# Decoding the input weights at fixed units of the attention loop, value half first

## The chip, the core and the metric

The kernel runs on one core of a Trainium2 chip. Its time is the device time of one execution in microseconds (us). The kernel before took 809.89 us in the median of three runs (809.17 to 810.18).

## What is computed

Attention with a block mask over 4 batches of 8 heads (576 positions, head size 64), then a gated feed-forward with a spatial mixing step, then a normalised second feed-forward with a residual. Only the first product of the second step matters for this change: `x @ w_in`, whose columns are two halves. Columns 0 to 511 give `u`, here called the **gate half**, columns 512 to 1023 give `v`, the **value half**.

```python
def _moe_ref(x, w_in, w_spatial, b_spatial, w_out):
    h = np.maximum(x @ w_in, 0.0)
    u, v = (h[..., :d_ff // 2], h[..., d_ff // 2:])
    ...
    gated = u * v_s
    return (gated @ w_out).astype(np.float32)
```

[...]

## The kernel before

**Units and pairs.** The attention works on 16 pairs of heads, four to a batch, numbered 0 to 15. Each pair is nine units of 64 or 128 query rows: the joint last rows of both heads first (i = 0), then blocks of 512, 384, 256 and 128 key columns, one for each head (i = 1 to 8). The main loop (L513) runs over the unit number u = 9 p + i, so the first batch is u = 0 to 35 and the second u = 36 to 71. A unit traces its score products (L214 and on, three PSUM banks), the mask and row minimum on VectorE (DVE, L275), the exponential on ScalarE (ACT, L282); two units later the transposes of the result on TensorE (PE, L333) and their evictions (DVE L324 for the wide units, ACT L326 for the others). At i = 7 a pair's weighted sum over the first part of the transposes is traced (`pv` from `pH`, L386, 20 matmuls), at i = 2 of the next pair the rest (`pv` from `pL`, 8 matmuls). At i = 0 the reciprocals of the previous pair are traced (DVE L292 and L293, PE L295, ACT L297). From i = 1 on, the next pair's `stack` operands are prepared (DVE L55 or ACT L57, and GpSimd, POOL, L188 or L196 to L202).

**The dense work.** From u = 44 on, the loop also deals out the products `x @ w_in` of the batch before, a few matmuls a unit (`fill`, L488): first four or five tiles of the value half (`vps`, L431), then four blocks of the gate half (`ups`, L462).

**Decoding w_in.** `win` holds `w_in` as a high and a low float32 part, in four row blocks `kc`. `decode_in` (L402) is a generator; each `next` on it traces one of eight parts, 128x512 numbers each: an activation that reads the high words (ACT L87), a shift of the low words (DVE L88), their joining (DVE L89), then a rounding copy (POOL L100) and a subtraction (POOL L101) into `win`. The loop calls it at L536 to L538, at i = 1, 4 and 7 of the first four pairs: the first call (u = 1) starts three fetches, the next eight (u = 4, 7, ... 25) trace the parts, and each part starts the fetch of the third part on (L409, a 512 KB transfer on SyncE's, SP's, queue) into one of three `raw` buffers.

**What sets the order.** The program is traced in source order, but a planner that simulates the engines (`schedule_with_timeline_sim=True`) then chooses each engine's order: an instruction may be brought forward when its inputs are there and its engine is idle in the simulation. `tc.keep_in_program_order` limits this: the instruction is not brought ahead of the one that was traced just before it on its engine. It does not hold back anything that is traced later. `decode` has a parameter `here` for it, which marks L87 and L88; `decode_in` does not use it.

Of the kernel before, what the change touches and what calls it, by code (L numbers as in the profile page):

```python
# [18 lines left out]

PLAN = {'mm': 3, 'sc': 3, 'tr': 2, 'D': 2, 'hi0': 'v', 'hi1': 's', 'klo0': 'g', 'klo1': 'g', 'qlo0': 'g', 'qlo1': 'g', 'xm0': 'g', 'xm1': 'g', 'xh0': 'g', 'xh1': 'g', 'xl0': 'g', 'xl1': 'g', 'dm': 'g', 'dh': 'g', 'ev0': 3, 'ev1': 2, 'rate': 24500.0, 'vrb': 3, 'ds': 2, 'dy': 1, 'raw': 5, 'yn': 2, 'ts': 3, 'ring': 8, 'wt': 2, 'cb': 1, 'hq': 8, 'packed': 4, 'plain': 3, 'pre': 8, 'py': 10, 'pyn': 4, 'dn0': 2, 'dnn': 5, 'vl': 'v', 'pace': 3, 'wd': 7, 'tl0': 'v', 'tl1': 'v', 'xe': 's', 'pt': 6, 'dstart': 8}  # L20


def f32(ap):
    return ap.bitcast(F32)
# [8 lines left out]
def tile_kernel(  # L33
# [26 lines left out]
    NB, NP, _, _, _, S = qk.shape  # L60
    KD = w_in.shape[1]
    DM = 128 * KD
    F = w_in.shape[2] // 2
# [14 lines left out]
    wi32, wo32, w132, w232 = (a.bitcast(U32) for a in (w_in, w_out, w_ch1, w_ch2))  # L78

    def decode(raw, m, e, out, here=lambda ins: ins):  # L80

        low, high = raw[:, :, 0], raw[:, :, 1]
        here(nc.scalar.activation(m, f32(high), AF.Prelu, scale=2.0**-112, alpha=2.0**32))  # L87
        here(nc.vector.tensor_scalar(e, low, 29, None, op0=ALU.logical_shift_right))  # L88
        nc.vector.scalar_tensor_tensor(  # L89
            out.bitcast(U32), m.bitcast(U32), 3, e, op0=ALU.logical_shift_left, op1=ALU.bitwise_or  # L90
        )

    def split(src, hi, lo, high="s", low="g"):

        if high == "s":
            nc.scalar.copy(hi, src)  # L96
        elif high == "v":
            nc.vector.tensor_copy(hi, src)
        else:
            nc.gpsimd.tensor_scalar(hi, src, 1.0, 0.0, op0=ALU.mult, op1=ALU.add)  # L100
        {"v": nc.vector, "g": nc.gpsimd}[low].tensor_tensor(lo, src, f32(hi), op=ALU.subtract)  # L101
# [164 lines left out]
    def softmax(u):  # L266

        j, c = UNITS[u % NU]
        banks = state[u]
        sm = sums[u // NU]  # L270
        pt = at.tile([128, S], F32, tag="p", name="p", bufs=PLAN['pt'])
        nm = at.tile([128, 2], F32, tag="nm", name="nm", bufs=4)
        for i, (s_ps, o, n) in enumerate(banks):
            m = mask[:, 0:n] if c == 4 else mask[:, 512 - n:512]
            nc.vector.tensor_tensor_reduce(  # L275
                pt[:, o:o + n], s_ps[:, :n], m, -0.125, 3e38, ALU.add, ALU.min, nm[:, i:i + 1]
            )
        if c == 4:
            nc.vector.tensor_tensor(nm[:, 0:1], nm[:, 0:1], nm[:, 1:2], op=ALU.min)
        n = o + n  # L280
        col = 8 if c == 4 else 4 * j + c
        nc.scalar.activation(  # L282
            pt[:, :n], pt[:, :n], AF.Exp, bias=nm[:, 0:1], scale=-1.0, accum_out=sm[:, col:col + 1]
        )
        state[u] = (pt, n)
# [31 lines left out]
    def transposes(u):  # L317
        j, c = UNITS[u % NU]
        pt, n = state.pop(u)

        def put(src, dst):
            out = dst(pT_of(u // NU)[1 if c >= 2 else 0])
            if c >= PLAN["ev1" if u >= NU * NP else "ev0"] and not (c == 4 and PLAN["tl1" if u >= NU * NP else "tl0"] == "s"):
                nc.vector.tensor_copy(out, src)  # L324
            else:
                nc.scalar.copy(out, src)  # L326

        def flip(k0, k1):
            tr = p_tr.tile([128, 512], F32, tag="tr", name="tr")
            for kc in range(k0, k1):  # L330
                w = min(128, n - 128 * kc)
                o = 128 * (kc - k0)
                nc.tensor.transpose(tr[:w, o:o + 128], pt[:, 128 * kc:128 * kc + w], idn)  # L333
            return tr

        if c == 4:
            tr = flip(0, 4)
            put(
                tr.rearrange("p (r h q) -> p r h q", h=2, q=64),
                lambda t: view(t, 256, [[WH, 4], [5 * WH, 2], [1, 64]]),  # L340
            )
            tr = flip(4, 5)
            put(
                tr[0:64, 0:128].rearrange("p (h q) -> p h q", q=64), lambda t: t[0:64, :, 4 * WH + 256:5 * WH]
            )
        else:
            tr = flip(0, c + 1)
            put(
                tr[:, :n].rearrange("p (r q) -> p r q", q=128),
                lambda t: view(  # L350
                    t, (5 * WH if c >= 2 else 2 * WL) * j + 128 * (c % 2), [[WH if c >= 2 else WL, c + 1], [1, 128]]
                ),
            )
# [5 lines left out]
    def tick():  # L359
        for e in list(slow):  # L360
            e[0] -= 1
            if e[0] <= 0:
                slow.remove(e)
                e[1]()

    def flush():
        todo, later[:] = list(later), []
        for f in todo:
            f()

    def weighted(p, part):

        flush()
        vt = ops[p][2]
        if p not in xx_t:
            xx_t[p] = at.tile([128, S], F32, tag="xx", name="xx")
        xx = xx_t[p]

        jobs = ((0, 128, 0, WL), (1, 128, 128, WL)) if part == 0 else (
            (0, 128, 0, WH), (1, 128, 0, WH), (2, 128, 0, WH), (3, 128, 128, WH), (4, S - 512, 256, WH))  # L380
        w = WH if part else WL
        src = pT_of(p)[part]
        ps = p_mm.tile([128, 512], F32, tag="mm", name="pv")
        for n, (kc, rows, a, z) in enumerate(jobs):
            for j in (1, 0):
                MM(  # L386
                    ps[64 * j:64 * j + 64, a:z], lhsT=vt[:rows, kc, 64 * j:64 * j + 64],
                    rhs=src[:rows, j, w * kc + a:w * kc + z],
                    start=(n == 0), stop=(n == len(jobs) - 1),
                )  # L390
        later.append(lambda: cp('xe', None, xx[:, 256 * part:256 * part + w], ps[:, :w]))
# [8 lines left out]
        del ops[p]  # L400

    def decode_in():  # L402
        raws = {}

        def fetch(i):
            if i < 2 * KD:
                kc, h = divmod(i, 2)
                raws[i] = dn.tile([128, F, 2], U32, tag="hl", name="raw", bufs=3)
                nc.sync.dma_start(  # L409
                    out=raws[i].rearrange("p a b -> p (a b)"), in_=wi32[:, kc, 2 * F * h:2 * F * h + 2 * F]  # L410
                )

        fetch(0)
        fetch(1)
        fetch(2)
        yield
        for i in range(2 * KD):
            kc, h = divmod(i, 2)
            m = dn.tile([128, F], F32, tag="vr", name="dm", bufs=PLAN["vrb"])
            e = dn.tile([128, F], U32, tag="ur", name="de")  # L420
            cols = slice(F * h, F * h + F)
            decode(raws.pop(i), m, e, m)
            split(m, win[0][:, kc, cols], win[1][:, kc, cols], PLAN['dh'])
            fetch(i + 3)
            yield
# [57 lines left out]
    dense = None  # L483
    debt = 0.0
    dec = decode_in()
    preps = {}

# [22 lines left out]
    size = [200 + (S if c == 4 else 128 * (c + 1)) for _, c in UNITS]  # L510
    tot = float(sum(size) * NP)
    D = PLAN['D']
    for u in range(NS + 8):  # L513
        p, i = divmod(u, NU)
        if u < NS:
            scores(u)
            softmax(u)
        tick()
        flush()
        if D <= u < NS + D:  # L520
            transposes(u - D)
        if i == PLAN['wd'] and p < NPAIR:
            weighted(p, 1)
        if i == 0 and 1 <= p <= NPAIR:
            reciprocals(p - 1)
        if i == D and 1 <= p <= NPAIR:
            weighted(p - 1, 0)
        if i == D + 3 and 1 <= p <= NPAIR:
            store_x(p - 1)
        if i == 0:  # L530
            load(p + 2)
            if p + 1 < NPAIR:
                preps[0] = prepare(p + 1)
        if 0 in preps and i >= 1:
            next(preps[0], None)
        if p < NP:  # L536
            if i % PLAN['pace'] == 1:
                next(dec, None)  # L538
        else:
            b, k = divmod(u, NU * NP)  # L540
            if k == PLAN['dstart'] and b <= NB - 1:
                dense = chain(dense, w_in_stage(b - 1))
            fill(PLAN['rate'] * size[i] / tot)
# [81 lines left out]
    dec = decode_out()  # L625
# [24 lines left out]
    raws = {}  # L650
# [441 lines left out]
def _layout(np, q, k, v, moe_w_in, moe_w_spatial, moe_b_spatial, moe_w_out, moe2_g_ln, moe2_w_ch1, moe2_w_ch2):  # L1092

    B, H, S, D = q.shape
    qk = np.stack([q, k], axis=2).reshape(B, H // 2, 2, 2, S, D).transpose(0, 1, 5, 2, 3, 4)
# [40 lines left out]
```

## Time and profile before

| | us |
|---|---|
| median of three runs | 809.89 |
| lowest and highest | 809.17, 810.18 |
| the profiled execution, its time | 811.71 |
| the profiled execution, first to last instruction | 809.9 |
| PE busy | 790.8 (98%) |
| DVE, ACT, POOL busy | 525.8, 423.9, 415.5 |

The profile lists, for each instruction, its engine, its line, what it writes and reads, when it started, how long it took and, where the engine sat idle before it, what ended that wait. PE is called busy while a matmul is in its pipeline, so a busy PE says little of its pace. The profile also records TensorE's granted clock, as a share of 2.4 GHz; 0.50 is 1.2 GHz. Before the first such record a stretch is shown as 1.00.

### The profile page before, as it was taken

The numbers are of one execution on the slowest core, as the hardware profiler recorded it, in microseconds if no ns is written. First come the engines' busy times: TensorE is split into PE (matmuls) and PEld (weight loads), VectorE is DVE, ScalarE is ACT, GpSimd is POOL, SyncE is SP. The second block draws the span as 40 slices with busy tenths as digits, with TensorE's granted clock in tenths as the row PEclk, the third lists the DMA queues.
The fourth block names the chain that finished last, engine by engine and source line by source line (L and its number), as shares of the span: only waits on it lengthen the run. The fifth ranks groups of instructions, "written<-read, shape, count | busy, mean of one in ns | idle before, by whom it ended". The sixth has DMA issues, their size and how long they took to land.

```text
span 809.9 us, 13259 instructions
## 1 busy us (share of the span) xinstructions
PE 790.8 (98%) x4480; PEld 672.9 (83%) x4480; DVE 525.8 (65%) x1191; ACT 423.9 (52%) x1071; POOL 415.5 (51%) x417
## 2 busy tenths in 40 slices
PE   7999999999999999999999999999999999999998
PEld 4667788868878799899988888889898888988986
DVE  5857655665465196786676788797556578645534
ACT  4678677657665264455363555463345454433431
POOL 5979655655452353232176455564555555545431
PEclk9899999999999999999999999999999999999999
DMA  8645535445342368778620243204001003000002
GB/s 250 179 133 165 155 115 160 142 130 153 110 149 73 114 206 280 233 241 262 205 79 14 79 128 106 80 1 156 1 13 40 1 1 126 18 1 1 1 1 78
DMA packets 53687, 88.66 MB, mean 109 GB/s; under 512 B 6770, under 2 KB 17138, under 8 KB 53620
## 3 DMA queue, kind: packets, MB, share of 16 engines
q1 hardware_dynamic: 53620, 87.83, 35.5%
q8 instruction: 35, 0.57, 0.3%
q14 instruction: 32, 0.26, 0.1%
HBM read 68.85 MB, written 18.95 MB: 108 GB/s over the span
## 4 chain that ended last, share of the span: by engine, by line
PE 84%; DVE 6%; DMA 3%; POOL 2%; issue 2%; ACT 2%; SPq 1%; POOLq 0%; ACTq 0%; DVEq 0%
PE hps L915 21%; PE o L105 8%; PE o L107 8%; PE o L106 8%; PE pv L386 6%; PE tr L333 5%; PE sc L260 4%; PE ups L105 2%; PE by L105 2%; PE by L107 2%; PE by L106 2%; PE sps L107 2%; PE sps L106 2%; PE sps L105 2%; PE ups L106 2%
## 5 line engine op out<-in xcount | busy, mean ns | idle before, releaser
L101 POOL TENSOR_TENSOR a<-s,a 128x256 fp32r<-128x256 f32 x96 | 78.3, 819 | 91.7 <-ACT a L96 91.7
L106 PE MATMUL o<-w,h 128*128 128x512 f32 x288 | 112.9, 393 | 0.0
L275 DVE CUSTOM_DVE_ANT_0 p<-sc,mask 128x256 f32<-128x256 f32 (+4 forms) x160 | 74.0, 472 | 56.8 <-PE tr L333 17.9
L105 PE MATMUL o<-w,h 128*128 128x512 f32 x288 | 107.8, 398 | 1.0 <-ACT h L907 1.0
L921 DVE TENSOR_TENSOR c<-hps,c 128x384 f32<-128x384 f32 x120 | 66.5, 554 | 54.4 <-PE hps L915 52.9
L282 ACT ACTIVATE p<-p,nm 128x384 f32<-128x384 f32 (+3 forms) x144 | 83.8, 583 | 31.8 <-DVE nm L275 29.1
L107 PE MATMUL o<-w,h 128*128 128x512 f32 x288 | 97.6, 397 | 0.1
L101 POOL TENSOR_TENSOR a<-w,a 128x256 fp32r<-128x256 f32 x72 | 60.4, 842 | 44.7 <-ACT a L96 39.2
L96 ACT CAST a<-s 128x256 fp32r<-128x256 f32 x96 | 38.4, 404 | 83.7 <-PE hps L915 76.9
L333 PE MATMUL tr<-idn,p 128*128 128x128 f32 (+1 forms) x400 | 72.0, 293 | 3.6 <-DVE pH L324 3.2
L324 DVE COPY pH<-tr 128x512 f32<-128x512 f32 (+1 forms) x88 | 49.5, 572 | 26.2 <-PE tr L333 25.9
L105 PEld LDWEIGHTS o<-w,h 128*128 128x128 f32 x288 | 53.7, 188 | 11.8 <-ACT h L907 2.3
L333 PEld LDWEIGHTS tr<-idn,p 128*128 128x128 f32 (+1 forms) x400 | 49.2, 146 | 16.6 <-issue 4.6
L106 PEld LDWEIGHTS o<-w,h 128*128 128x128 f32 x288 | 54.1, 188 | 10.1
L107 PEld LDWEIGHTS o<-w,h 128*128 128x128 f32 x288 | 53.2, 188 | 8.8 <-DVE h L908 1.0
L765 POOL TENSOR_TENSOR gt<-gf,gt 128x576 fp32r<-128x576 f32 (+1 forms) x17 | 24.5, 1442 | 61.5 <-ACT gt L764 61.5
L200 POOL TENSOR_TENSOR stack<-qkt,stack 64x576 fp32r<-64x576 f32 x24 | 34.2, 1427 | 42.2 <-ACT stack L57 41.5
L116 POOL TENSOR_TENSOR rs<-rs,nhalf 128x1 f32<-128x1 f32 x36 | 23.4, 651 | 51.8 <-DVE rs L115 51.4
L908 DVE SCALAR_TENSOR_TENSOR h<-c,h 128x384 fp32r<-128x384 f32 x72 | 46.5, 666 | 1.6 <-ACT h L907 1.5
L260 PE MATMUL sc<-stack 128*128 128x512 f32 (+3 forms) x192 | 45.4, 344 | 0.4 <-DVE nm L275 0.2
L87 ACT ACTIVATE dm<-raw 128x256 f32<-128x256 f32 (+1 forms) x72 | 32.1, 463 | 26.1 <-DVE w L89 6.0
L907 ACT ACTIVATE h<-c 128x384 fp32r<-128x384 f32 x72 | 35.3, 521 | 16.7 <-DVE c L921 16.4
(174 smaller groups left out, 2224.6 us busy)
## 6 DMA issues: line engine op xcount, KB each, us to landing
raw<-in_w_ch_dram SPq DMA_DIRECT2D x64, 256.0 KB
qkt<-in_qk_dram SPq DMA_DIRECT2D x112, 144.0 KB
vt<-in_v_dram SPq DMA_DIRECT2D x16, 320.0 KB
rb<-r_d SPq DMA_DIRECT2D x32, 144.0 KB
u_d<-ur SPq DMA_DIRECT2D x16, 288.0 KB
us<-u_d SPq DMA_DIRECT2D x16, 288.0 KB
y_d<-ys SPq DMA_DIRECT2D x18, 256.0 KB
yr<-y_d SPq DMA_DIRECT2D x18, 256.0 KB
```

What stands on the lines that cost most here:

```text
L101: {"v": nc.vector, "g": nc.gpsimd}[low].tensor_tensor(lo, src, f32(hi), op=ALU.subtract)
L105: MM(out_ps, lhsT=a[0], rhs=b[0], start=first, stop=False)
L106: MM(out_ps, lhsT=a[0], rhs=b[1], start=False, stop=False)
L107: MM(out_ps, lhsT=a[1], rhs=b[0], start=False, stop=last)
L260: MM(s_ps[:, :nn], lhsT=st[:, j, i, q], rhs=st[:, j, 2, 0:nn], start=(i == 0), stop=(i == 1))
L275: nc.vector.tensor_tensor_reduce(pt[:, o:o + n], s_ps[:, :n], m, -0.125, 3e38, ALU.add, ALU.min, nm[:, i:i + 1])
L282: nc.scalar.activation(pt[:, :n], pt[:, :n], AF.Exp, bias=nm[:, 0:1], scale=-1.0, accum_out=sm[:, col:col + 1])
L324: nc.vector.tensor_copy(out, src)
L333: nc.tensor.transpose(tr[:w, o:o + 128], pt[:, 128 * kc:128 * kc + w], idn)
L386: MM(ps[64 * j:64 * j + 64, a:z], lhsT=vt[:rows, kc, 64 * j:64 * j + 64], rhs=src[:rows, j, w * kc + a:w * kc + z], start=(n == 0), stop=( ...
L915: MM(ps, lhsT=a[x], rhs=b[y], start=not more and kc == 0 and k == 0, stop=kc == KD // 2 - 1 and k == 2, skip_group_check=True,)
L921: nc.vector.tensor_tensor(out, ps, x, op=ALU.add)
```

## The change

Three things change in how `w_in` is decoded. The parts are taken in another order: the four row blocks of the value half, then the four of the gate half, where before the two halves of each row block followed one another. L87 and L88 are traced with `tc.keep_in_program_order`. And the calls come at nine listed units: u = 4 starts the first fetches, u = 9, 13, 17, 21, 25 and 29 trace six parts, u = 49 and 54 (the fifth unit of pair 5 and the first of pair 6, in the second batch) trace the last two, row blocks 2 and 3 of the gate half.

```diff
@@ decode_in
         def fetch(i):
             if i < 2 * KD:
-                kc, h = divmod(i, 2)
+                h, kc = divmod(i, KD)
                 raws[i] = dn.tile([128, F, 2], U32, tag="hl", name="raw", bufs=3)
                 nc.sync.dma_start(
-                    out=raws[i].rearrange("p a b -> p (a b)"), in_=wi32[:, kc, 2 * F * h:2 * F * h + 2 * F]
+                    out=raws[i].rearrange("p a b -> p (a b)"), in_=wi32[:, kc, 2 * F * (1 - h):2 * F * (2 - h)]
                 )
...
         for i in range(2 * KD):
-            kc, h = divmod(i, 2)
+            h, kc = divmod(i, KD)
             m = dn.tile([128, F], F32, tag="vr", name="dm", bufs=PLAN["vrb"])
             e = dn.tile([128, F], U32, tag="ur", name="de")
-            cols = slice(F * h, F * h + F)
-            decode(raws.pop(i), m, e, m)
+            cols = slice(F * (1 - h), F * (2 - h))
+            decode(raws.pop(i), m, e, m, tc.keep_in_program_order)
             split(m, win[0][:, kc, cols], win[1][:, kc, cols], PLAN['dh'])
             fetch(i + 3)
             yield
@@ the main loop
+    DECODE = (4, 9, 13, 17, 21, 25, 29, 49, 54)
...
-        if p < NP:
-            if i % PLAN['pace'] == 1:
-                next(dec, None)
-        else:
+        if u in DECODE:
+            next(dec, None)
+        if p >= NP:
             b, k = divmod(u, NU * NP)
```

## Rows read from the trace of the kernel before

**Rows 1.** Stretches: length, busy us (instructions) by engine, clock, DMA share, GB/s.

```profile
core 0: us, PE busy (x) PEld busy (x) DVE busy (x) ACT busy (x) POOL busy (x), PEclk, DMA share, GB/s
13.65:31.75 18.10, 18.10 (x69) 11.71 (x68) 16.41 (x40) 12.74 (x35) 15.78 (x13) 1.00 0.92 262
31.75:35.16 3.41, 2.92 (x18) 1.89 (x17) 2.33 (x7) 2.05 (x8) 2.11 (x3) 1.00 0.88 192
35.16:41.99 6.83, 6.62 (x31) 5.35 (x31) 6.23 (x15) 3.41 (x12) 6.20 (x5) 0.50 0.25 73
41.99:53.43 11.44, 11.44 (x80) 7.43 (x79) 5.68 (x22) 9.04 (x24) 7.64 (x10) 1.00 0.54 128
53.43:65.24 11.81, 11.81 (x87) 8.05 (x86) 7.17 (x28) 10.53 (x31) 10.81 (x11) 1.00 0.42 122
91.80:98.33 6.53, 5.81 (x36) 4.73 (x36) 5.30 (x14) 2.41 (x7) 6.30 (x7) 1.00 0.37 119
```

**Rows 2.** Transposes of L333: durations ns min/median/max, from 12 to 31, then 42 to 66.

```profile
L333 PE MATMUL tr<-idn,p x22: 415/418/473, 13.6 to 30.8; 128*128 128x128 f32 x21, 128*64 128x128 f32 x1
L333 PE MATMUL tr<-idn,p x51: 271/273/421, 41.6 to 66.0; 128*128 128x128 f32 x49, 128*64 128x128 f32 x2
```

**Rows 3.** In order of time (start, us, what): PE and DVE after the first rise.

```profile
33.45 0.62 PE L254 MATMUL sc<-stack 64*128 64x256 f32 x3 [0.29 <-DVE nm L275]
35.37 0.96 PE L254 MATMUL sc<-stack 64*128 64x192 f32 x3 [0.27 <-DVE nm L275]
...
33.31 0.69 DVE L89 SCALAR_TENSOR_TENSOR dm<-dm,de 128x512 uint32<-128x512 uint32 x1
34.39 0.60 DVE L88 TENSOR_SCALAR de<-raw 128x512 uint32<-128x512 uint32 x1
```

**Rows 4.** PE in order of time: weighted sums and the next pairs' 512-column scores.

```profile
26.31 4.52 PE L386 MATMUL pv<-pH,vt 128*64 128x320 f32 x20
42.88 0.97 PE L254 MATMUL sc<-stack 64*128 64x512 f32 x3
45.05 2.42 PE L386 MATMUL pv<-pH,vt 128*64 128x320 f32 x20
55.31 1.49 PE L254 MATMUL sc<-stack 64*128 64x512 f32 x9
```

**Rows 5.** The eight parts' five instructions: durations ns min/median/max, first and last start.

```profile
L87 ACT ACTIVATE dm<-raw x8: 643/670/696, 15.5 to 35.6; 128x512 f32<-128x512 f32 x8
L88 DVE TENSOR_SCALAR de<-raw x8: 409/714/1589, 13.9 to 34.4; 128x512 uint32<-128x512 uint32 x8
L89 DVE SCALAR_TENSOR_TENSOR dm<-dm,de x8: 672/684/1418, 16.3 to 38.6; 128x512 uint32<-128x512 uint32 x8
L100 POOL TENSOR_SCALAR win<-dm x8: 616/761/1116, 17.1 to 42.2; 128x512 fp32r<-128x512 f32 x8
L101 POOL TENSOR_TENSOR win<-dm,win x8: 1270/1378/2797, 17.9 to 45.9; 128x512 fp32r<-128x512 f32 x8
```

**Rows 6.** In order of time: reciprocal copies, an eviction, a wait, the first gate block.

```profile
34.67 0.24 ACT L297 COPY rr<-rps 9x128 f32<-9x128 f32 x1
...
94.72 0.65 DVE L324 COPY pH<-tr 128x512 f32<-128x512 f32 x1
...
98.33 0.41 PE L333 MATMUL tr<-idn,p 128*128 128x128 f32 x2 [0.72 <-DVE pH L324]
...
104.32 0.25 ACT L297 COPY rr<-rps 9x128 f32<-9x128 f32 x1
...
108.14 0.40 PE L105 MATMUL ups<-xT,win 128*128 128x288 f32 x1
```

**Rows 7.** Waits of SP's queue, 0 to 130: us in total, times, longest.

```profile
SPq L409 <- DVE de L88: 6.9, 2, 4.0
```

**Rows 8.** POOL's last preparation for pair 5, and pair 5's first scores on PE.

```profile
69.20 1.41 POOL L202 TENSOR_TENSOR stack<-qkt,stack 64x576 fp32r<-64x576 f32 x1
...
76.73 0.72 PE L239 MATMUL sc<-stack,qtail 128*128 128x256 f32 x4
```

## The prediction

> **What bounds the kernel now.** I read the busy shares first: PE is busy nearly throughout (the table above), so only stretches where PE waits or runs at the low clock can give time back. Then the busy time by stretch for the first two batches, then PE in order of time. The reader is to see three things.
>
> First, PE is at its low clock for most of the first 42 us. From 13.65 to 31.75 the clock stands as 1.00 [rows 1] only because no record came before; the transposes there take 418 ns, and from 42 on 273 ns [rows 2]. At 31.75 the clock rises, from 35.16 to 41.99 it is 0.50 (1.2 GHz) again, and after that it stays at 1.00 (2.4 GHz) [rows 1]. While the clock is low PE is busy all the time: 18.10 of 18.10 us from 13.65 to 31.75 [rows 1], although DVE (16.41) and POOL (15.78) are full of decoding there. So decoding costs PE next to nothing before 31.75.
>
> Second, the clock fell at 35.16 after the one stretch in which it was high and PE was not full: 2.92 of 3.41 us busy [rows 1]. What PE waited for there is the row minimum, 0.29 us and 0.27 us [rows 3], and between two row minima DVE did decoding, a joining of 0.69 us and a shift of 0.60 us [rows 3]. The same pieces of the next pair keep the clock: 11.44 of 11.44 us at 1.00 [rows 1].
>
> Third, what this is worth. From the start of the weighted sum to the next pair's first 512-column scores, pair 1's work takes 42.88 - 26.31 = 16.57 us and the next pair's 55.31 - 45.05 = 10.26 us [rows 4], 6.31 us less.
>
> **What the change moves.** In the kernel before the planner brought the parts forward: traced at u = 4 to 25, their shifts ran from 13.9 to 34.4 and their last subtraction started at 45.9 [rows 5]. Pinned, a part's shift and activation cannot come before what was traced just ahead of them. Placed on the trace of before:
> - Part 0 (u = 9): its activation stands behind pair 0's reciprocal copy on ACT, 34.67 [rows 6]. Parts 1 and 2 (u = 13, 17) stand behind evictions of u = 11 and u = 15, and fall into the stretch that starts at 41.99 [rows 1].
> - Parts 3 to 5 (u = 21, 25, 29) fall into the stretch that starts at 53.43 [rows 1].
> - Part 6 (u = 49): its shift stands behind the eviction of u = 47, which I take to be the copy at 94.72 [rows 6].
> - Part 7 (u = 54): its activation stands behind pair 5's reciprocal copy at 104.32 [rows 6]; its shift behind that pair's reciprocals on DVE, still in the stretch from 91.80.
>
> So no part but the first is left before 35, two stand where DVE, ACT and PE share the waits of 92 to 98, and nothing of the computation is removed. One part costs DVE 0.41 to 1.59 us and 0.68, ACT 0.67, POOL 0.76 and 1.38 (up to 1.12 and 2.80) [rows 5].
>
> **The gain.** Of the 6.31 us I leave out what comes before the rise: the sum itself, 4.52 against 2.42 us, 2.10 [rows 4], and half of the 0.92 us from its end to 31.75, 0.46. There remain 3.75 us. From the other side: 6.83 us at half clock are worth 3.42, and PE's gaps of 31.75 to 35.16 are 3.41 - 2.92 = 0.49 [rows 1], 3.91 together. I take 3.8, if the clock holds; if it falls as before, only the 0.5 of the gaps.
>
> **The costs.**
> - Part 0 in 34 to 38, the gap it leaves behind a row minimum: between 0 and one joining, 0.68; I take 0.2, since ACT has 1.36 us free in 31.75 to 35.16 and 3.42 in the next stretch [rows 1].
> - Parts 1 to 5 at the high clock. DVE has 5.76 and 4.64 us free in the two stretches from 41.99 and 53.43, ACT 2.40 and 1.28 [rows 1]. Two parts ask of ACT 1.34 in the first, three ask 2.01 in the second: 0.73 more than is free. On DVE three parts ask 3 x (0.71 + 0.68) = 4.2 of 4.64. Bounds: 0 (all hidden, PE full in both stretches) and 5 x 0.5 (each as the two waits of [rows 3] with their part); I take 0.7, ACT's excess.
> - Parts 6 and 7 on DVE in 91.80 to 98.33. PE is busy 5.81 of 6.53 us there, and its wait of 0.72 ends on a DVE copy [rows 1, 6]. DVE has 1.23 us free; part 6 and part 7's shift ask (0.71 + 0.68) + 0.71 = 2.1, with the longest shifts 3.9. Bounds 0 (the dense matmuls fill the gap) and 2.7, the longest less what is free; I take 1.0, about 2.1 less 1.23.
> - Part 7 and the first gate block: 104.32 + 0.25 + 0.67 + 0.68 + 0.76 + 1.38 = 108.1, and the block starts at 108.14 [rows 6], with row block 3 last of four. Cost 0, as long as POOL is free; if POOL's longest durations apply, 1.8 later, of which PE does other work first.
> - DMA and SP's queue: the same eight transfers. SP's queue stood 6.9 us, twice, for a raw buffer [rows 7], with the loads of later pairs behind it; the later fetches wait longer each, but a pair's loads have a whole pair (10 us and more, [rows 4]) before they are used. 0; the cover is that pair's length, and a miss would show as PE waiting for `stack`.
> - The order of the halves and the list of units themselves cost nothing: the value half is wanted after u = 44, the gate half after the value tiles.
>
> Sum: -3.8 + 0.2 + 0.7 + 1.0 = **-1.9 us**. Against the profiled execution that is 811.71 - 1.9 = 809.8; that execution lay 1.8 above the median of 809.89, so for the median I give **808.0 us**. All later stages are held by PE or start when this one has ended, so I let the gain pass to the end whole.
>
> **Two rules of the Trainium skill.** POOL's subtraction takes 1.27 us at best and 2.80 at worst, the shift 0.41 and 1.59 [rows 5]. The Trainium skill ("GPSIMD Engine Reference", 8. Key points) says why such a spread can be: GpSimd shares its SBUF interfaces with VectorE, and contends with VectorE instructions in a two-port mode or with two SBUF inputs. That speaks against the change: it moves three parts to a stretch where POOL is busy 10.81 of 11.81 us [rows 1], and by it each part there would cost DVE the long durations. What that gives is the third rival below.
>
> The transposes' pace followed the clock [rows 2], and the stretch that lost the clock held transposes and short scores [rows 3]. The Trainium skill ("TensorE: Matmul & The Clock Gate", Part 4: PE-mode transpose) says that transposes don't count as PE being busy for the clock. By it less decoding might not hold the clock at 35.16, which is the second rival; the same pieces one pair later kept it [rows 1], which speaks for the forecast.
>
> **Rivals.**
> 1. *The clock rises earlier.* The rise at 31.75 came in the run of the 20 weighted sums and what follows, which began at 26.31 [rows 4]. With ACT and DVE free the planner may put that sum earlier, and the sum would then run at 2.4 GHz in good part: up to 2.10 more, I take 1.7: 806.3. For it: DVE's 16.41 of 18.10 us falls [rows 1]. Against it: PE had no gap there, so only another order on PE can do it.
> 2. *The clock falls all the same.* Then only the gaps come back: -0.5 + 1.9 = +1.4: 811.3. For it: the score loop still has three banks and the same chain. Against it: 11.44 us of the next pair at 1.00 [rows 1].
> 3. *POOL becomes the bound* (slower). Parts 3 to 5 ask POOL for 3 x 2.14 = 6.4 us, at the long durations 3 x 3.92 = 11.8, and POOL has 1.00 free [rows 1, 5]. The last preparation of pair 5 ends at 70.61, its first score starts at 76.73: 6.1 us of cover [rows 8]. At the median the backlog is 5.4 and hidden; at the long durations it is 10.8 and 4.7 us late at pair 5. It decides when the three parts take POOL more than 7.1 us. Then -1.9 + 4.7 = +2.8: 812.7.
> 4. *The change does not do what it says in time*: the pins hold ACT's and DVE's instructions only, the planner fills the freed time with other work, and the clock's gain and the second batch's cost cancel: 809.9.
>
> **How the numbers follow.** Forecast 0.45, with its own range 806.3 to 809.4 (costs 0 to about 3.3); rival 1 0.16; rival 2 0.20; rival 3 0.09; rival 4 0.10. From no cost and the earlier rise (809.9 - 3.8 - 1.7 = 804.4) to rival 3's full price the range is 804.6 to 812.4, which leaves out the extremes of both. About 0.2%, 1.6 us, is what a measurement of this kernel can tell from no change: faster is below 808.3. The forecast falls there with two thirds, rival 1 nearly whole: 0.30 + 0.15 = 0.45, and 0.02 of the others; same takes a third of the forecast, rival 4 and most of rival 2: 0.15 + 0.10 + 0.11 = 0.36; slower the rest, 0.17.
>
> **What would show it.** Right: in the profile after, a clock of 1.00 from the first rise on with no second stretch of 0.50 before 60 us; pair 1's span from weighted sum to the next 512-column scores near 12.8 us; no L88 or L89 before 25; the waits of 92 to 98 longer by about 1 us. Wrong: 0.50 again after the first rise (rival 2); PE waiting for `stack` near 75 (rival 3); the first `ups` later against `vps`, or PE waiting for `win` (part 7); a changed order on PE ahead of the first weighted sum (rival 1). The forecast as a whole is wrong if the clock's gain is there and the stages after 300 us take it back.

## The result, and the profile after

The changed kernel takes 816.49 us in the median (814.83 to 818.65), the kernel before 809.99 us beside it: the ratio is 1.0085 [1.0069, 1.0101], 6.5 us slower. The forecast was 808.0 us with a range of 804.6 to 812.4, so the time lies 4.1 us above the range. The profiled execution of after took 817.06 us, 815.3 from first to last instruction, against 811.71 and 809.9.

Decoding makes one float32 of the two 32-bit words in which each 64-bit weight reaches the kernel: the activation (L87) reads the high word, the shift (L88) brings three bits of the low word into place, and the joining (L89) puts the two together.

I read TensorE (PE) first, in order of time, at the places of [rows 4]: each pair's weighted sum and the next 512-column scores, and two later waits. Start, length, what; the last line is pair 4's first scores in the kernel before:

```profile
24.52 2.42 PE L386 MATMUL pv<-pH,vt 128*64 128x320 f32 x20
35.50 0.97 PE L254 MATMUL sc<-stack 64*128 64x512 f32 x3
37.68 0.96 PE L254 MATMUL sc<-stack 64*128 64x512 f32 x3 [1.21 <-DVE nm L275]
...
53.23 0.90 PE L333 MATMUL tr<-idn,p 128*128 128x128 f32 x3 [1.24 <-DVE pH L324]
54.06 1.65 PE L254 MATMUL sc<-stack 64*128 64x512 f32 x3
...
71.11 0.71 PE L260 MATMUL sc<-stack 128*128 128x512 f32 x2
...
102.87 0.44 PE L333 MATMUL tr<-idn,p 128*128 128x128 f32 x2 [1.89 <-DVE pH L324]
...
67.05 1.17 PE L260 MATMUL sc<-stack 128*128 128x512 f32 x4
```

Pair 1's weighted sum takes 2.42 us instead of 4.52, and pair 2's first 512-column scores start at 35.50 instead of 42.88: **7.4 us ahead** of the kernel before. Pair 3's start at 54.06 instead of 55.31, so 6.1 us of that are gone one pair later; pair 4's start at 71.11 instead of 67.05, 4.1 us behind. The gain was real, larger than forecast, and lost twice over between 35.5 and 71.

Second, the stretches between the changes of the granted clock (the first, as in [rows 1], stands before any record):

```profile
core 0: us, PE busy (x) PEld busy (x) DVE busy (x) ACT busy (x) POOL busy (x), PEclk, DMA share, GB/s
13.65:22.51 8.86, 8.86 (x39) 7.37 (x39) 6.68 (x25) 5.24 (x18) 3.02 (x3) 1.00 0.67 179
22.51:46.41 23.90, 21.43 (x139) 13.57 (x139) 16.11 (x44) 17.17 (x54) 14.12 (x14) 1.00 0.71 188
46.41:49.82 3.41, 3.41 (x18) 2.43 (x17) 1.34 (x5) 3.03 (x7) 3.20 (x4) 0.50 0.22 57
49.82:53.23 3.41, 1.68 (x12) 1.19 (x11) 3.41 (x7) 0.86 (x3) 3.26 (x3) 1.00 0.78 234
53.23:60.06 6.83, 6.83 (x21) 3.48 (x23) 4.85 (x15) 4.67 (x13) 3.90 (x7) 0.50 0.35 116
60.06:104.43 44.37, 40.59 (x274) 30.66 (x270) 28.93 (x92) 29.64 (x84) 36.17 (x31) 1.00 0.48 129
104.43:107.84 3.41, 3.41 (x15) 1.62 (x16) 3.41 (x5) 1.96 (x5) 2.63 (x3) 0.50 0.52 146
```

The clock rises at 22.51 instead of 31.75, and it falls three times to 0.50 (1.2 GHz), for 13.65 us in all, where in [rows 1] it stood at 1.00 from 41.99 to 65.24 and from 91.80 to 98.33. Ahead of each fall PE was not full: the row from 49.82 shows it best, PE busy 1.68 of 3.41 us while VectorE (DVE) is busy for all of it.

Third, what PE waited for from 30 to 120 us (total, times, longest), and beneath it the same waits of the kernel before:

```profile
PE tr L333 <- DVE pH L324: 4.4, 3, 1.9
PE sc L254 <- DVE nm L275: 1.5, 2, 1.2
PE sc L235 <- DVE nm L275: 0.5, 1, 0.5
...
PE tr L333 <- DVE pH L324: 1.0, 2, 0.7
PE sc L254 <- DVE nm L275: 0.6, 2, 0.3
```

Here `pH` stands for evictions and `nm` for row minima. Fourth, DVE in order of time where the 1.21 us wait at 37.68 arises, and beneath it GpSimd (POOL) at the same time:

```profile
33.92 0.69 DVE L324 COPY pH<-tr 128x512 f32<-128x512 f32 x1
34.53 0.71 DVE L88 TENSOR_SCALAR de<-raw 128x512 uint32<-128x512 uint32 x1
35.16 0.28 DVE L275 CUSTOM_DVE_ANT_0 p<-sc,mask 128x128 f32<-128x128 f32 x1
...
35.37 1.92 DVE L88 TENSOR_SCALAR de<-raw 128x512 uint32<-128x512 uint32 x1
37.21 0.41 DVE L275 CUSTOM_DVE_ANT_0 p<-sc,mask 128x256 f32<-128x256 f32 x1
...
37.96 1.71 DVE L89 SCALAR_TENSOR_TENSOR dm<-dm,de 128x512 uint32<-128x512 uint32 x1
...
39.66 0.68 DVE L275 CUSTOM_DVE_ANT_0 p<-sc,mask 128x512 f32<-128x512 f32 x1
...
33.53 2.98 POOL L188 TENSOR_TENSOR stack<-qkt,stack 128x576 fp32r<-128x576 f32 x2
37.69 1.43 POOL L396 TENSOR_TENSOR xx<-xx,rb 128x576 f32<-128x576 f32 x1 [0.68 <-DMA rb<-r_d]
```

In 33.92 to 39.66 DVE stands idle at no point, and 4.34 us of it are two shifts and a joining. PE waits to make the next scores, and the row minima that it waits for stand behind the decode. The same figure (two shifts with a row minimum between them, then an eviction) makes the 1.24 us wait for `pH` at 53.23. Over all, the shift's longest rose from 1.59 to 1.92 us and the joining's from 1.42 to 1.71 [rows 5].

### The profile page after: what moved, and what is told of

Read it like the earlier page. It is cut to its first block, busy times and chain, and to the rows that moved or that the text cites. A ratio compares the mean times of both kernels' runs of the same rounds, so it can differ in the third digit from the quotient of the medians.

```text
span 815.3 us, 13238 instructions
## 1 busy us (share of the span) xinstructions
PE 789.6 (97%) x4480; PEld 671.1 (82%) x4480; DVE 531.9 (65%) x1191; ACT 423.5 (52%) x1071; POOL 413.6 (51%) x417
## 4 chain that ended last, share of the span: by engine, by line
PE 82%; DVE 8%; DMA 3%; issue 2%; ACT 2%; POOL 1%; SPq 0%; POOLq 0%; ACTq 0%; DVEq 0%
PE hps L916 21%; PE o L105 8%; PE o L107 8%; PE o L106 8%; PE pv L386 6%; PE tr L333 5%; PE sc L260 4%; PE ups L105 2%; PE sc L254 2%; PE ups L106 2%; PE ups L107 2%; PE by L105 2%; PE by L107 1%; PE by L106 1%; PE vps L105 1%
## 5 line engine op out<-in xcount | busy, mean ns | idle before, releaser
L333 PE MATMUL tr<-idn,p 128*128 128x128 f32 (+1 forms) x400 | 70.9, 290 | 8.0 <-DVE pH L324 6.8
L324 DVE COPY pH<-tr 128x512 f32<-128x512 f32 (+1 forms) x88 | 49.4, 574 | 31.8 <-PE tr L333 31.4
L333 PEld LDWEIGHTS tr<-idn,p 128*128 128x128 f32 (+1 forms) x400 | 48.6, 145 | 20.1 <-DVE pH L324 5.8
L200 POOL TENSOR_TENSOR stack<-qkt,stack 64x576 fp32r<-64x576 f32 x24 | 35.2, 1467 | 28.2 <-ACT stack L57 27.7
L396 POOL TENSOR_TENSOR xx<-xx,rb 128x576 f32<-128x576 f32 x16 | 22.8, 1426 | 47.9 <-DMA rb<-r_d 37.1
L87 ACT ACTIVATE dm<-raw 128x256 f32<-128x256 f32 (+1 forms) x72 | 31.9, 464 | 24.9 <-DVE w L89 7.7
```

## The experiments

Ratios are against the kernel before, run on the same chip beside them.

### The units without the pins, the pins without the units

The changed kernel without its pins (a_nopin):

```diff
-            decode(raws.pop(i), m, e, m, tc.keep_in_program_order)
+            decode(raws.pop(i), m, e, m)
```

> The changed kernel without its two pins; halves' order and units stay. Theory 'pins': the units alone move nothing, since the planner brings every part forward to where an engine is free, so all eight shifts run before 45 us, the second batch has none, and the time is that of the kernel before: 808 to 812 us. Theory 'units': decoding later is what costs, whoever sets the order: 814 to 818 us, with shifts left near 97 to 101 us.

Measured: 810.61 us, 0.999 [0.9975, 1.0004]. All eight shifts lie at 13.9 to 32.9 us again, as in [rows 5], because the planner brings them forward. Two joinings stay behind, at 89.24 and 100.42, so the list of units moves a little, and the time does not change. The profile also shows what the parts do at the high clock: here it rose at 18.40, and PE then waited 3.70 us for a row minimum that stands behind a joining and a shift on DVE:

```profile
29.26 1.74 DVE L89 SCALAR_TENSOR_TENSOR dm<-dm,de 128x512 uint32<-128x512 uint32 x1
31.04 0.43 DVE L88 TENSOR_SCALAR de<-raw 128x512 uint32<-128x512 uint32 x1
31.38 0.55 DVE L275 CUSTOM_DVE_ANT_0 p<-sc,mask 128x384 f32<-128x384 f32 x1
...
31.99 0.98 PE L254 MATMUL sc<-stack 64*128 64x256 f32 x3 [3.70 <-DVE nm L275]
```

The kernel before with the pins alone (b_pin):

```diff
-            decode(raws.pop(i), m, e, m)
+            decode(raws.pop(i), m, e, m, tc.keep_in_program_order)
```

> The kernel before with the two pins alone; its units (every third of the first batch) and its order of halves stay. Theory 'pins': the shifts stand behind evictions and row minima in the stretches at the high clock and PE waits for DVE there: 812 to 818 us. Theory 'units': 808 to 812 us, since no part is traced in the second batch.

Measured: 810.59 us, 0.9996 [0.9986, 1.0007], a miss for the theory that pins cost wherever they stand. In its profile pair 2 starts early (33.5 us, as after) and PE then waits 3.9 us for `nm` and 2.2 us for `pH`: a gain and a loss that cancel. The pins make the trade; the units and the order of the halves, which no run takes apart, decide its balance. That the order of the halves makes the loss by itself is ruled out by c_slot5 below, which keeps it and is faster than both kernels.

The changed kernel with its last two parts in the first batch (a_all1):

```diff
-    DECODE = (4, 9, 13, 17, 21, 25, 29, 49, 54)
+    DECODE = (4, 9, 13, 17, 21, 25, 29, 33, 34)
```

> The changed kernel with its last two parts traced at u = 33 and 34, in the first batch, in place of u = 49 and 54. Theory 'second batch': the shifts and joinings at 97 to 102 us cost a wait of 1.9 us and half of a 3.4 us stretch at 0.50, less what the parts cost earlier: 812 to 814 us. Theory 'anywhere': a pinned part costs as much in the first batch: 815 to 818 us.

Measured: 816.71 us, 1.0073 [1.005, 1.0097], as the change. So the two parts that the change sets in the second batch are not needed for the loss; set into the first, they cost about the same.

### Leaving out VectorE's part of the decode

The changed kernel with ScalarE's activation alone, still pinned (a_nodve):

```diff
-            e = dn.tile([128, F], U32, tag="ur", name="de")
...
-            decode(raws.pop(i), m, e, m, tc.keep_in_program_order)
+            tc.keep_in_program_order(nc.scalar.activation(m, f32(raws.pop(i)[:, :, 1]), AF.Prelu, scale=2.0**-112, alpha=2.0**32))
```

> The changed kernel without DVE's part of decoding w_in (the shift and the joining are left out, so the low bits of the weights are missing); ACT's pinned reading and POOL's split stay where they are. Theory 'DVE': the shifts and joinings, stretched by POOL's two-input work, make PE's waits (4.4 us for evictions, 2.0 us for row minima) and through them the clock's falls: with them gone the clock stays at 1.00 after its rise near 22 us and the time is 802 to 807 us. Theory 'order': the pins' order on ACT and POOL costs as much: 812 us or more.

Measured: 802.33 us, 0.9889 [0.9871, 0.9907]; the three bits that the joining adds are left out of every part. Its PE rows at the same places, and one stretch:

```profile
24.46 2.42 PE L386 MATMUL pv<-pH,vt 128*64 128x320 f32 x20
35.15 0.96 PE L254 MATMUL sc<-stack 64*128 64x512 f32 x3
...
47.42 1.48 PE L254 MATMUL sc<-stack 64*128 64x512 f32 x9
...
59.43 1.17 PE L260 MATMUL sc<-stack 128*128 128x512 f32 x4
...
22.68:110.00 87.32, 85.29 (x582) 61.58 (x581) 59.99 (x187) 67.62 (x195) 70.35 (x65) 1.00 0.59 162
```

The clock rises as early as in the changed kernel; this one starts pair 2 at the same time, has no fall of the clock, and goes through pairs 2 and 3 in 24.28 us (35.15 to 59.43) where the changed kernel takes 35.61 (35.50 to 71.11): 11.3 us. ScalarE's and GpSimd's shares of the decode are still there, ScalarE's pinned as in the change, and GpSimd still waits 11.3 us for the decode's activations (15.8 for the joinings in the change, both up to 115 us). So what the change loses, it loses by the two instructions on DVE.

The same for parts 0 to 5 alone (a_only67):

```diff
-            decode(raws.pop(i), m, e, m, tc.keep_in_program_order)
+            if i < 6:
+                tc.keep_in_program_order(nc.scalar.activation(m, f32(raws.pop(i)[:, :, 1]), AF.Prelu, scale=2.0**-112, alpha=2.0**32))
+            else:
+                decode(raws.pop(i), m, e, m, tc.keep_in_program_order)
```

> The changed kernel without VectorE's two instructions (L88, L89) for parts 0 to 5; parts 6 and 7 of the gate half keep theirs (low bits of six parts of w_in are left out). This takes the two joined terms of the sum apart. As forecast, parts 6 and 7 would cost 1.0 us (bounds 0 to 2.7) over the 802.3 us of the kernel without any of VectorE's decode: 803.3 us (802.3 to 805). If the shifts at 97 and 101 that stand before the new scores' row minima and the late joining at 111 cost as much as those at 35 to 68 (about 14 us for eight parts, two of eight): 805 to 807 us. If they cost most of it through the clock's fall at 104: 809 to 813 us.

Measured: 806.22 us, 0.9946 [0.9931, 0.9962]. Against a_nodve the ratio is 0.0057 higher: parts 6 and 7 cost 4.6 us, parts 0 to 5 the other 11.3 (0.0139). The time lies in the second expectation's 805 to 807; the forecast had 1.0 for parts 6 and 7. With nothing of DVE's decode before them they stand at 87.4 to 98.4 us here, and PE waits 1.39 us for `pH` at 107.41, with 3.42 us of half clock from 108.41.

### The shift or the joining

The changed kernel without the shift (a_no88): the joining takes the raw words, with an and in place of the or, and is pinned in this kernel, which it is not in the change.

```diff
-            decode(raws.pop(i), m, e, m, tc.keep_in_program_order)
+            raw = raws.pop(i)
+            tc.keep_in_program_order(nc.scalar.activation(m, f32(raw[:, :, 1]), AF.Prelu, scale=2.0**-112, alpha=2.0**32))
+            tc.keep_in_program_order(nc.vector.scalar_tensor_tensor(
+                m.bitcast(U32), m.bitcast(U32), 3, raw[:, :, 0], op0=ALU.logical_shift_left, op1=ALU.bitwise_and
+            ))
```

> The changed kernel without the shift L88: the joining takes the raw words as its second operand (the low bits come out wrong), everything else stands as in the change. Theory 'shift in front' (the shift waits for nothing but its load, stands in pairs ahead of row minima, and is what delays them): most of the 14 us between 802.3 and 816.5 goes, 803 to 808 us. Theory 'busy time' (each instruction costs what it takes; L88 takes 0.84 and L89 0.89 us at the median): about half goes, 808 to 811 us. Theory 'joining waits' (the joining holds VectorE while ScalarE makes dm): little goes, 812 to 816 us.

Measured: 805.34 us, 0.9925 [0.9897, 0.9953], 2.9 us over a_nodve (0.0036, give or take 0.0033). Its profile does not put them down to the joinings. The one long wait of PE goes back over ScalarE and GpSimd to a load (`rb`), and the clock is at 0.50 for 6.83 us behind it, from 56.64:

```profile
52.78 1.43 POOL L396 TENSOR_TENSOR xx<-xx,rb 128x576 f32<-128x576 f32 x1 [2.28 <-DMA rb<-r_d]
55.57 0.40 ACT L204 CAST qtail<-stack 128x256 fp32r<-128x256 f32 x1 [2.44 <-POOL stack L200]
56.30 0.28 PE L295 MATMUL rps<-idn,sm 128*9 128x128 f32 x1 [2.19 <-ACT pL L326]
```

The changed kernel without the joining (a_no89):

```diff
-            decode(raws.pop(i), m, e, m, tc.keep_in_program_order)
+            raw = raws.pop(i)
+            tc.keep_in_program_order(nc.scalar.activation(m, f32(raw[:, :, 1]), AF.Prelu, scale=2.0**-112, alpha=2.0**32))
+            tc.keep_in_program_order(nc.vector.tensor_scalar(e, raw[:, :, 0], 29, None, op0=ALU.logical_shift_right))
```

> The changed kernel without the joining L89: the shift L88 is made and not used (the low three bits of w_in's low halves are left out). Theory 'shift in front': little goes, 811 to 816 us. Theory 'busy time': about half goes, 808 to 811 us. Theory 'joining waits': most goes, 803 to 808 us.

Measured: 810.3 us, 0.9999 [0.9974, 1.0023]: the shifts alone cost 8.9 us (0.0110) over a_nodve. The waits of the change stand at the same places again, which they do not in a_no88:

```profile
37.65 0.95 PE L254 MATMUL sc<-stack 64*128 64x512 f32 x3 [1.22 <-DVE nm L275]
...
52.92 0.90 PE L333 MATMUL tr<-idn,p 128*128 128x128 f32 x3 [1.25 <-DVE pH L324]
```

Together the two cost 15.9 us (0.0196), 4 us more than the sum of each alone, which by the intervals is barely clear of noise. Both instructions take nearly the same time in the change (0.84 and 0.89 us in the median), so busy time does not explain that the shifts cost 6 us more than the joinings. What I take to be the reason, and have not shown, is where they stand: the shift needs nothing but its load and so is put ahead of row minima and evictions whose inputs are not ready yet in the plan; the joining needs ScalarE's activation and is placed later. "Shift in front" named 803 to 808 for the one, which came, and 811 to 816 for the other, which missed by 0.7; "busy time" holds for the second alone. The 4 us are open: I take them for the crowd that both make.

### GpSimd's two-input instructions

L188, L200, L202, L396 and L398 of pairs 0 to 5 with one input (a_pool1); two of the five:

```diff
+                if p < 6:
+                    nc.gpsimd.tensor_scalar(st[:, 1, i, :], raw[:, 0, i], 0.0, 0.0, op0=ALU.mult, op1=ALU.add)
+                else:
                     E("klo",p).tensor_tensor(st[:, 1, i, :], raw[:, 0, i], hi[:, i], op=ALU.subtract)
...
+        if p < 6:
+            nc.gpsimd.tensor_scalar(xx, xx, 1.0, 0.0, op0=ALU.mult, op1=ALU.add)
+        else:
             E('xm', p).tensor_tensor(xx, xx, rb_t.pop(p), op=ALU.mult)
```

> The changed kernel with GpSimd's two-input instructions of pairs 0 to 5 (the low parts of the stacks, the weighting by the reciprocal sums, the low part of x) replaced by one-input instructions of the same size (low parts and the reciprocals of those pairs are left out). Theory 'GpSimd's two-input instructions stretch VectorE's shifts and joinings': the longest L88 falls from 1.92 to 0.7 us or less, the longest L89 from 1.71 to 0.9 or less, VectorE's clumps at 34 to 38 and 50 to 53 shrink by some 3 us, and the time goes to 806 to 811 us. Rival 'order alone' (the place in VectorE's order costs, the stretching doesn't): 814 to 818 us with the durations down. If the durations stay as they are, the stretching has another cause.

Measured: 814.73 us, 1.0068 [1.0042, 1.0094]. The durations after, and a stretch of its profile, without any fall of the clock:

```profile
L88 DVE TENSOR_SCALAR de<-raw x8: 367/686/1256, 23.9 to 97.4; 128x512 uint32<-128x512 uint32 x8
L89 DVE SCALAR_TENSOR_TENSOR dm<-dm,de x8: 687/836/1205, 33.4 to 106.0; 128x512 uint32<-128x512 uint32 x8
...
29.31:110.00 80.69, 76.34 (x507) 54.69 (x505) 57.45 (x178) 58.92 (x169) 49.25 (x59) 1.00 0.60 155
```

The longest fell from 1.92 to 1.26 us and from 1.71 to 1.21, not to the 0.7 and 0.9 expected, and the time is that of "order alone", its interval overlapping the change's: the ratio is 0.0017 lower, 1.4 us, give or take 2.5. So GpSimd's two-input instructions stretch DVE's, and by the times most of the loss stays without that. Where it stays, the one profile doesn't say. Its clock rises only at 29.31 and then never falls; pair 2 starts at 36.55 (33.26 in the change), and pairs 2 to 4 take 39.6 us from there, against 46.9 in the change and 36.3 in a_nodve, with no wait of PE over 0.6 us. So this execution lost at its start what the change loses later, and how much of the change's waits is the stretching stays open.

### The kernel before, once more

> The kernel before once more, for its clock records alone. If the first rise of the clock (31.75 us in the profiled execution of before, 22 to 23 us in the three kernels whose parts were held back) is set by the kernel, it comes at 30 us or later again; if it is the chip's own phase, it may come anywhere from 18 to 32 us. The time is that of before, 808 to 812 us.

Measured: 811.28 us, 809.4 first to last. The clock rises at 31.40, near the 31.75 of before, but does not fall at 35:

```profile
31.40:35.16 3.76, 3.32 (x24) 2.20 (x23) 1.87 (x6) 2.21 (x7) 2.83 (x3) 1.00 0.99 255
35.16:41.99 6.83, 5.06 (x38) 3.86 (x39) 6.83 (x17) 4.51 (x17) 6.11 (x6) 1.00 0.57 158
...
27.35 4.37 PE L386 MATMUL pv<-pH,vt 128*64 128x320 f32 x20
...
42.20 0.95 PE L254 MATMUL sc<-stack 64*128 64x512 f32 x3
```

This is the forecast's gain without the change, and it is worth little: from the weighted sum to the scores 42.20 - 27.35 = 14.85 us against 16.57 [rows 4], and pair 2's scores start 0.7 us earlier (42.20 against 42.88). With the clock up, DVE is busy all of 35.16 to 41.99 (two joinings of 1.42 and 1.34 us among it) and PE only 5.06 of 6.83. The 86 timed runs of the kernel before say the same: nine whose mean granted clock was 0.999 or more have a median of 809.53 us, seven with 0.992 or less 811.66, the rest 810.80. By this some 2 us go with all the falls of the clock in a run, where I had counted 3.8 on one of them.

### Where in the pair the parts stand

The changed kernel with the call right behind the unit's softmax, ahead of its transposes, and other units (c_slot):

```diff
-    DECODE = (4, 9, 13, 17, 21, 25, 29, 49, 54)
+    DECODE = (1, 6, 9, 11, 20, 29, 38, 47, 56)
...
             softmax(u)
+        if u in DECODE:
+            next(dec, None)
         tick()
...
-        if u in DECODE:
-            next(dec, None)
```

> The changed kernel with the same pins, but the units of the decode chosen otherwise: the loads start at unit 1, parts 0 and 1 stand in units 6 and 9 (slow-clock stretch of the start), and the other six one to a pair, directly behind the row minima of the second 512-column scores (units 11, 20, 29, 38, 47, 56). There VectorE stood idle for 0.83 and 2.13 us in pairs 3 and 4 of the kernel without VectorE's part of the decode, because TensorE makes the pair's late pv. Theory 'order on VectorE' (a part costs what it delays of row minima and evictions, not its busy time): nearly all of the cover is there; 803 to 807 us, clock 1.00 from about 22 to 100, waits of TensorE for nm and pH under 0.7 us each. Rival 'busy time' (eight parts take about 1.1 to 1.4 us each of an engine that has none to give, wherever they lie): 810 to 816 us. Rival 'clock phase' (the time follows where the chip lets the clock fall, which the place of the parts doesn't set): 808 to 812 us.

Measured: 807.8 us, 0.9964 [0.994, 0.9987]: faster than both kernels, just above the 803 to 807 expected. In its profile it takes 35.8 us from the first scores of pair 2's joint rows (37.1 us) to those of pair 5 (72.9), a_nodve 36.3 (33.3 to 69.6): three parts at no cost. What this execution lost against a_nodve's lies in pair 1, where the clock fell at 30.06 for 6.83 us.

The same call, other units (c_slot2):

```diff
-    DECODE = (1, 6, 9, 11, 20, 29, 38, 47, 56)
+    DECODE = (1, 6, 11, 20, 29, 38, 47, 51, 56)
```

> The kernel of the run c_slot with its part of unit 9 (which stood with that of unit 11 in VectorE's order at 24.7 to 29.2 us, where the clock then fell at 30.06) taken away and a part set in unit 51 instead: parts in units 6, 11, 20, 29, 38, 47, 51 and 56. Theory 'order on VectorE': in c_slot the spans of pairs 2 to 5 (12.4, 12.4, 11.0, 15.8 us) were already those of the kernel without VectorE's decode (12.2, 12.1, 12.0, 16.5), and what was left was the crowd of two parts in pair 1 with the fall of the clock behind it (pair 2 begins at 37.1 instead of 33.3 us, 3.8 us). Without it 803 to 806 us. Rival 'clock phase' (the fall at 30 us came by itself): 806 to 809 us, as c_slot.

Measured: 809.47 us, 0.9989 [0.9976, 1.0002]: a miss for both, though the interval overlaps c_slot's. Here a joining of 1.20 us at 65.4 made PE wait 0.59 us for `nm` in pair 4, where it stands one row minimum later on DVE than in c_slot. The last part's joining, at 101.44, itself waited 0.46 us for ScalarE's activation with a row minimum behind it, and PE waited 1.92 us for that at 102.66. The clock fell behind each.

The same call, other units (c_off):

```diff
-    DECODE = (1, 6, 9, 11, 20, 29, 38, 47, 56)
+    DECODE = (1, 6, 15, 24, 33, 42, 47, 51, 56)
```

> The kernel of the run c_slot2 with four parts moved by four units, from behind the row minima of the second 512-column scores (units 11, 20, 29, 38) to behind the softmax of the second 256-column scores (units 15, 24, 33, 42): still one part to a pair, the same pins, the same number, but L88 now stands ahead of an eviction of pH (L324) and L89 beside the row minima and evictions of the 128-column units. Theory 'order on VectorE': each of the four costs 1 to 3 us again, 808 to 814 us, with TensorE waiting for pH or nm over 0.7 us in pairs 1 to 4. Rival 'spread' (what helped in c_slot is one part to a pair and no crowd, wherever it stands): the time of c_slot2 within 1.5 us.

Measured: 811.2 us, 1.0008 [0.9992, 1.0023], 1.7 us above c_slot2 with intervals that overlap: in the range of "order" and 0.2 us outside that of "spread", so the time alone does not decide. The profiles are further apart: pairs 2 to 4 take 42.2 us (34.5 to 76.8), in c_slot2 38.2 (34.1 to 72.3). The place shows in its rows, DVE and then PE:

```profile
34.06 1.39 DVE L88 TENSOR_SCALAR de<-raw 128x512 uint32<-128x512 uint32 x1
35.37 0.68 DVE L324 COPY pH<-tr 128x512 f32<-128x512 f32 x1
...
36.11 0.55 PE L333 MATMUL tr<-idn,p 128*128 128x128 f32 x3 [0.97 <-DVE pH L324]
```

One shift ahead of one eviction, and PE waits 0.97 us for that eviction.

The same call, other units (c_slot5):

```diff
-    DECODE = (1, 6, 9, 11, 20, 29, 38, 47, 56)
+    DECODE = (1, 4, 7, 11, 20, 29, 38, 47, 56)
```

> The kernel of the run c_slot with parts 0 and 1 in units 4 and 7 instead of 6 and 9, so that no two parts stand together in pair 1; the other six behind the second 512-column row minima as in c_slot. If c_slot's gain of 0.4% comes from its order, this has it too: 804 to 808 us. If it was luck of the clock or of the neighbourhood, 808 to 811 us, as c_slot2.

Measured: 807.59 us, 0.9964 [0.9949, 0.9979]: c_slot's gain again, without its crowd. In pair 3 the shift stands where DVE has no row minimum or eviction to make, while PE is busy with the weighted sum:

```profile
50.69 2.42 PE L386 MATMUL pv<-pH,vt 128*64 128x320 f32 x20
51.46 0.63 DVE L275 CUSTOM_DVE_ANT_0 p<-sc,mask 128x512 f32<-128x512 f32 x1
...
52.01 1.02 DVE L88 TENSOR_SCALAR de<-raw 128x512 uint32<-128x512 uint32 x1
53.60 0.70 DVE L89 SCALAR_TENSOR_TENSOR dm<-dm,de 128x512 uint32<-128x512 uint32 x1 [0.56 <-POOL qtail L162]
54.21 0.56 DVE L275 CUSTOM_DVE_ANT_0 p<-sc,mask 128x384 f32<-128x384 f32 x1
```

With c_slot this is the version that beats both kernels, by 0.4% of the one and 1.2% of the other. 0.75% above a_nodve is left, 6.1 us for eight parts instead of the change's 15.9. In its profile the same three parts as in c_slot are not free: pairs 2 to 4 take 38.3 us (34.5 to 72.8), 2.0 more than in a_nodve, with c_slot2's order and its wait of 0.59 us in pair 4. The clock fell at 25.31 and at 69.68.

## Why the prediction was wrong, by its own steps

**What bounds the kernel.** "Decoding costs PE next to nothing before 31.75" holds for a PE at the low clock alone. In a_nopin the parts stand there too, the clock rose at 18.40, and PE waited 3.70 us for a row minimum at 31.99. A PE that is full at the low clock had hidden what the same parts cost at the high one. And "after that it stays at 1.00" holds for the rows shown: the trace of before has one more fall, at 345.77 for 3.41 us, and b_again one at 345.43.

**The gain, -3.8.** It came, and more of it: 7.4 us at pair 2's scores. From the start of the weighted sum to the first scores there are 35.50 - 24.52 = 10.98 us against 16.57 before. That is 5.6 less, the forecast's 3.8 and the first rival's 1.7 together, and it includes the sum itself at 2.42 us instead of 4.52. The other 1.8 us are that the sum started earlier, which neither priced. Rival 1's condition, a new order on PE ahead of the sum, was not the point (the order there is the same but for three score matmuls): an earlier rise was. But the fall at 35.16, by itself, was not what cost: b_again has none and, with the parts still in place, is 0.7 us ahead at pair 2's scores.

**Part 0, 0.2.** Not contradicted: its shift stands at 20.77, earlier than forecast, and its joining of 0.69 us at 30.24, and no wait of PE follows before 37.68. No run takes this part out alone.

**Parts 1 to 5, 0.7 with bounds 0 to 2.5.** This is the step that failed. Against a_nodve pairs 2 and 3 cost 11.3 us. In pair 2 (18.56 us against 12.27) PE's waits of 0.3 us and more are 1.21, 0.45, 0.39, 0.40, 0.49 and 1.24, 4.2 us together, where a_nodve has none, and 4.24 us at half clock are worth up to 2.1: 6.3 of 6.3. In pair 3 (17.05 against 12.01) it is the rest of the half clock, 6.0 us worth up to 3.0, and 1.6 of waits: 4.6 of 5.0. I had summed DVE's free time by stretch (5.76 and 4.64 us) and found the parts to fit. But free time is in pieces, and the pieces are where PE is late already; a shift of 0.7 to 1.9 us ahead of a row minimum or an eviction delays PE by what the three score banks don't cover, whatever is free two microseconds later. And the upper bound of 2.5 went by two waits of the kernel before, at the end of 3.41 us at the high clock: no bound on the same parts beside a PE that is at the high clock for 23.9 us. Even all three upper bounds together (0.7 + 2.5 + 2.7) give 812.0 us, so the measured time lies beyond them and not only beyond what was taken.

**Parts 6 and 7, 1.0 with bounds 0 to 2.7.** Mis-sized too: 4.6 us by a_only67. The place was as forecast (shifts at 96.6 and 100.7, joinings at 97.7 and 110.9), and the wait it lengthened too, from 0.72 to 1.89 us at 102.87. What the sum left out is the 3.41 us of half clock behind that wait, worth up to 1.7. With the 1.2 by which the wait grew that is 2.9 of the 4.6; where the rest arises is not shown.

**The costs taken as 0** held: in the profile PE never waits for `win` or for `stack`, from the first part to the last gate block. The third rival (a backlog on POOL, late for pair 5) did not happen.

**The second rival** (the clock falls all the same) happened, but not at 35 and not at the price named, +1.4. It was priced as if the rest stayed as in the kernel before; the falls came in pairs 2, 3 and 6, where the kernel before had none, behind the waits that the moved parts made. So waits and falls add up: 7.7 us of waits (4.2, 1.6 and 1.89) and up to 6.8 us of clock (half of 13.65) together at most 14.5, against a difference of 13.6 us between the spans of the changed kernel and a_nodve.

**The rule on GpSimd.** In 35.37 to 39.6 DVE's instructions took 1.92 and 1.71 us beside POOL's two-input instructions (L188 to 36.51, then L396 from 37.69), and in a_pool1, with one-input ones, at most 1.26 and 1.21. The Trainium skill ("GPSIMD Engine Reference", 8. Key points) has the two engines share SBUF interfaces and contend when VectorE's instruction has two SBUF inputs or runs in a two-port mode; the trace agrees for the joining. For the shift, which has one input, it would have to be the two-port mode; that it is stretched the rows show, in which mode it ran no run here does. I had spent the rule on a rival about POOL's backlog; it belonged into the durations of parts 1 to 5, as their upper end.

**The chances** leaned on one clock pattern of one execution as a thing that the change would remove. b_again shows that the kernel before has other patterns at the same time.

## What to carry to other kernels

An off-path instruction that waits for nothing but a load was the dearer one to move here (8.9 us against 2.9): look where it will stand in its engine's order, and what an engine on the path needs from the instructions behind it. Free time summed over a stretch is no cover; a gap at a known place is (here, DVE while PE makes the weighted sum: three parts cost nothing there in one profile and 2.0 us in another, where five elsewhere cost 11 us). And a fall of the clock in one profile is a draw: profile the same kernel twice before a gain is counted on its going away.

## What the chip showed that I had not expected

- The same 128x512 shift takes 0.37 to 1.93 us, the joining 0.63 to 1.89, in these profiles.
- The clock's first rise is not set by the instructions alone. c_slot and c_slot2 have the same instructions in the same order on TensorE, VectorE, ScalarE and GpSimd up to 24 us, and the first record of 1.00 comes at 23.24 us in the one and at 17.60 in the other. In the earlier one PE then waits 0.56 and 0.77 us for row minima, and the clock falls at 24.43 for 3.41 us.
- Two profiles of the kernel before have the rise at 31.4 and 31.75, those of the changed kernel, b_pin, a_nodve, a_all1, a_only67 and a_no88 at 22.1 to 23.2. But a_nopin, with the parts where the kernel before has them, rose at 18.40 (and fell at 32.06, for 10.24 us). a_no89 rose at 18.57 and a_pool1 at 29.31. So that holding the parts back brings the early rise is likely, and not shown.
